# A banded attention block and its dense layer: no branch ahead of the work, other PSUM banks for the first chunk, other due times

## The chip, the cores and the metric

One core of a Trainium2 chip. The metric is device microseconds (us) of one execution of the program. Most executions agree within 0.3%.

## The reference: what is computed

```python
# attention: q, k, v are (4, 8, 768, 64) float32; n_sink = 4, window = 128 (int64 scalars)
scores = q @ k.T / sqrt(64)
keep = (key < n_sink) | ((query - key >= 0) & (query - key < window))
a = softmax(where(keep, scores, -1e9))        # divided by the row sum + 1e-9
x = (a @ v), laid out as (3072, 512)
# dense layer: w_in (512, 2048) and w_out (2048, 512), float64
h = x @ w_in
out = ((h * cos(h)) @ w_out).astype(float32)
```

`n_sink` and `window` are known only when the program runs. The kernel has a fast path for 0 <= n_sink <= 8 and 1 <= window <= 128, and a general path for everything else.

## The kernel before, in words

**Tiling.** The 3072 tokens are 12 chunks of 256 (`NT`), each of one batch. Per chunk there are 8 heads of attention and then 8 dense slots. A slot is 256 of the 2048 columns of `w_in`: 24 products for h (L393, half 0 needs head pairs 0 and 1 of x, half 1 the pairs 2 and 3), the cosine chain on ACT and DVE (L402 to L432), and 12 products into the two output accumulators (L441). Numbers are carried as a high and a low part (`xhi`, `xlo`, `whi`, `wlo`), so each product is three matmuls. The first three chunks (one of each of three batches, 24 heads, `o.early`) do their attention in plain float32 on TensorE: transposes of q and k (`qk`, L736), scores (`s`, L760), masked copy with row minimum (`p`, L829), exponential (L838), scaling (L858), transposes of p (`tp`, L918), values (`av`, L948). The other chunks use split operands (L816, L972).

**Weights.** They are float64 in memory. 32 pieces of 512 KB are loaded into one of two `raw` buffers; DVE makes a float32 of each in three instructions (L494, L500, L506), ACT rounds it to the high part (L527), DVE or POOL subtracts for the low part (L530). 32 more loads later feed a range check (`check_piece`), whose result `redo` says at the very end whether the general path must run.

**The order of the work** is written out ahead of time by a planner (`Plan`). Each step has engines with a cost each, its dependencies, and a due time (`prio`, smaller goes first); `order` walks through time, gives each free engine its ready step with the smallest due time, and the result is emitted engine by engine. On the chip each engine then goes through its own list in that order and waits by semaphores. The due times are built from the table `C`: `head_time(g)` and `slot_time(a, s)` are the base times, `DQ`, `DS`, `DX`, `DV`, `DA` shift the steps of a head, `WI`, `WO`, `WS`, `LEAD` those of the weights, `CK` those of the range check. With `FILL`, 160 matmuls into an unused bank (`idle`, L1208) stand in the plan with the last due time of all, so they take TensorE's planned gaps.

**PSUM** has eight banks: `s` (scores), `tp`, `av`, `b3` (`qk`), `b0` and `b1` (output accumulators), `b4` and `b2` (h of the slots in turn; `b3` too from the third chunk on).

**The opening.** `setup` loads `n_sink` and `window` on SP's queue, makes the identity, iotas and 22 warm-up matmuls (11 in the source, each runs as two), and has DVE compute whether the limits suit the fast path (`flag`). The planner's clock has a gate at 5.4: the loads on SP, and DVE and ACT steps marked `ahead`, may stand before it. All else comes behind a branch on `flag`: every engine loads the flag into a register (L1407) and branches (L1408). Behind the branch DVE makes the masks (L1258 to L1266) in among its first steps, and POOL clears three tiles.

**The end.** DVE reduces the range check to `redo` (L1278 to L1282, with one transpose on TensorE, L1280), every engine loads it (L1411) and branches past the general path (L1412).

Of the kernel before, what the change touches and what calls it, by code (L numbers as in the profile page):

```python
# [16 lines left out]
P = 128  # L17
NSINK = 8
# [28 lines left out]
class Plan:  # L47
# [5 lines left out]
    def __init__(self):  # L53
        self.steps, self.bufs, self.port, self.ahead = [], {}, set(), set()
# [6 lines left out]
    def add(self, engines, fn, deps, prio, lat=0.0, table=None, port=False, ahead=False):  # L61
        self.steps.append((engines, fn, deps, prio, lat, table))
        if ahead:
            self.ahead.add(len(self.steps) - 1)
        if port:
            self.port.add(len(self.steps) - 1)
        return len(self.steps) - 1

    def order(self, gate=0.0):
# [22 lines left out]
        free = dict.fromkeys(ready, gate)  # L92
        free["SP"] = min(gate, 0.9)
        free["DVE"] = free["ACT"] = min(gate, C["PRE"])
# [4 lines left out]
        table, done, starts = None, [False] * n, []  # L99
# [3 lines left out]
        while left:  # L103
# [4 lines left out]
            for e, rs in ready.items():  # L108
# [60 lines left out]
        early = gate - 1e-6  # L169
        return [s for s in starts if s[0] < early], [s for s in starts if s[0] >= early]  # L170
# [3 lines left out]
def attn_moe_kernel(ctx, tc, q, k, v, n_sink, window, w_in, w_out, out):  # L174
# [439 lines left out]
    def banded_path():  # L614
# [513 lines left out]
        def after_softmax(g, o):  # L1128
# [8 lines left out]
            if o.early:  # L1137
# [8 lines left out]
                if o.odd == 0:  # L1146
                    x.bav = buf("av", 1)
# [298 lines left out]
```

## Time and profile before

| | |
|---|---|
| three runs | 768.08, 768.29, 772.59 us; median 768.29 |
| the profiled execution | 770.14 us, span of its instructions 768.7 us |
| granted TensorE clock, mean | 0.989 |
| busy: TensorE matmul / DVE / ACT / POOL | 740.4 / 610.1 / 579.1 / 140.4 us |
| chain that ended last | PE 79%, DVE 7%, ACT 6%, DMA 5%, issue 2% |

Busy TensorE time includes the 160 `idle` matmuls and the warm-up, which compute nothing. Matmuls are pipelined, so a group's time from start to start is the better price of one. `PEclk` is the granted clock as a share of 2.4 GHz.

### The profile page before, as it was taken

The numbers are of one execution on the slowest core, as the hardware profiler recorded it, in microseconds if no ns is written. First come the engines' busy times: TensorE is split into PE (matmuls) and PEld (weight loads), VectorE is DVE, ScalarE is ACT, GpSimd is POOL, SyncE is SP. The second block draws the span as 40 slices with busy tenths as digits, with TensorE's granted clock in tenths as the row PEclk, the third lists the DMA queues.
The fourth block names the chain that finished last, engine by engine and source line by source line (L and its number), as shares of the span: only waits on it lengthen the run. The fifth ranks groups of instructions, "written<-read, shape, count | busy, mean of one in ns | idle before, by whom it ended". The sixth has DMA issues, their size and how long they took to land.

```text
span 768.7 us, 15296 instructions
## 1 busy us (share of the span) xinstructions
PE 740.4 (96%) x5027; PEld 669.1 (87%) x5027; DVE 610.1 (79%) x1606; ACT 579.1 (75%) x1350; POOL 140.4 (18%) x234
## 2 busy tenths in 40 slices
PE   7998979999999999999999999999999999999995
PEld 6787858899998999988989999999998999999994
DVE  5888889867898989989989987987878978954431
ACT  2798885868888778788787788798789888874331
POOL 2120220000122222222222312221022212210000
PEclk8999999999999999999999999999999999999998
DMA  5575465221374376375275342322323222110000
GB/s 154 163 199 155 155 159 176 58 43 36 77 185 101 62 181 159 66 196 129 51 191 153 60 111 50 52 66 51 57 58 63 53 62 52 35 40 1 28 1 32
DMA packets 215674, 71.51 MB, mean 93 GB/s; under 512 B 204320, under 2 KB 204320, under 8 KB 215584
## 3 DMA queue, kind: packets, MB, share of 16 engines
q1 hardware_dynamic: 215584, 70.43, 38.0%
q8 instruction: 42, 0.69, 0.4%
q14 instruction: 48, 0.39, 0.2%
HBM read 64.10 MB, written 6.29 MB: 92 GB/s over the span
## 4 chain that ended last, share of the span: by engine, by line
PE 79%; DVE 7%; ACT 6%; DMA 5%; issue 2%; SPq 1%; DVEq 0%
PE h L393 30%; PE acc L441 29%; PE av L972 5%; PE tp L918 4%; PE s L816 4%; DMA xk<-in_k_dram 2%; PE av L948 2%; PE idle L1208 1%; ACT p L838 1%; PE s L760 1%; DMA v<-in_v_dram 1%; DVE p L829 1%; DMA xq<-in_q_dram 1%; PE gp L900 1%; DVE glo L432 1%
## 5 line engine op out<-in xcount | busy, mean ns | idle before, releaser
L393 PE MATMUL h<-xhi,whi_in 128*128 128x256 f32 x768 | 224.4, 292 | 3.9 <-DVE glo L432 3.9
L393 PE MATMUL h<-xlo,whi_in 128*128 128x256 f32 x768 | 216.3, 282 | 0.0
L393 PE MATMUL h<-xhi,wlo_in 128*128 128x256 f32 x768 | 216.0, 281 | 0.0
L393 PEld LDWEIGHTS h<-xhi,whi_in 128*128 128x128 f32 x768 | 145.1, 189 | 15.2 <-DVE glo L432 5.9
L441 PE MATMUL acc<-whi_out,ghi 128*128 128x512 f32 x384 | 155.8, 406 | 0.2
L393 PEld LDWEIGHTS h<-xhi,wlo_in 128*128 128x128 f32 x768 | 145.4, 189 | 7.9 <-issue 0.5
L441 PE MATMUL acc<-wlo_out,ghi 128*128 128x512 f32 x384 | 151.7, 395 | 0.2 <-DVE wlo_out L530 0.2
L441 PE MATMUL acc<-whi_out,glo 128*128 128x512 f32 x384 | 150.7, 392 | 0.0
L393 PEld LDWEIGHTS h<-xlo,whi_in 128*128 128x128 f32 x768 | 145.1, 189 | 0.0
L829 DVE CUSTOM_DVE_ANT_0 p<-s,mk 128x264 f32<-128x264 f32 (+1 forms) x192 | 75.9, 399 | 28.1 <-PE s L816 22.3
L838 ACT ACTIVATE p<-p,st 128x264 f32<-128x264 f32 (+1 forms) x192 | 93.5, 490 | 0.7
L432 DVE TENSOR_TENSOR glo<-h,ghi 128x512 fp32r<-128x512 f32 x96 | 65.7, 684 | 30.3 <-ACT ghi L426 29.5
L441 PEld LDWEIGHTS acc<-whi_out,glo 128*128 128x128 f32 x384 | 72.3, 188 | 16.4
L415 ACT ACTIVATE r<-r,neg 128x512 f32<-128x512 f32 x96 | 69.0, 723 | 20.4 <-DVE r L408 20.0
L441 PEld LDWEIGHTS acc<-whi_out,ghi 128*128 128x128 f32 x384 | 72.7, 189 | 5.4 <-DVE raw L384 0.5
L441 PEld LDWEIGHTS acc<-wlo_out,ghi 128*128 128x128 f32 x384 | 73.0, 190 | 4.8 <-DVE wlo_out L530 0.7
L420 DVE TENSOR_TENSOR h<-h,r 128x512 f32<-128x512 f32 x96 | 66.1, 690 | 14.0 <-ACT r L415 13.8
L408 DVE SCALAR_TENSOR_TENSOR r<-h,yt 128x512 f32<-128x512 f32 x96 | 65.4, 682 | 14.4 <-ACT yt L402 13.8
L426 ACT CAST ghi<-h 128x512 fp32r<-128x512 f32 x96 | 55.8, 581 | 27.7 <-PE acc L441 26.7
L402 ACT ACTIVATE yt<-h 128x512 int32<-128x512 f32 x96 | 57.2, 596 | 19.6 <-PE h L393 18.1
L871 POOL TENSOR_TENSOR vr<-v,vr 128x192 fp32r<-128x192 f32 (+1 forms) x57 | 33.8, 592 | 159.6 <-ACT vr L866 145.1
L816 PE MATMUL s<-r,l 128*128 128x264 f32 (+2 forms) x288 | 61.0, 292 | 0.2
(128 smaller groups left out, 1381.5 us busy)
## 6 DMA issues: line engine op xcount, KB each, us to landing
raw<-in_moe_w_in_dram SPq DMA_DIRECT2D x32, 512.0 KB
raw<-in_moe_w_out_dram SPq DMA_DIRECT2D x32, 512.0 KB
xk<-in_k_dram SPq DMA_DIRECT2D x256, 48.0 KB
out_dram<-raw SPq DMA_DIRECT2D x24, 256.0 KB
v<-in_v_dram SPq DMA_DIRECT2D x64, 96.0 KB
xq<-in_q_dram SPq DMA_DIRECT2D x144, 32.0 KB
v<-in_v_dram SPq DMA_DIRECT2D x32, 64.0 KB
xq<-in_q_dram SPq DMA_DIRECT2D x24, 64.0 KB
```

Source lines behind the costliest of these rows:

```text
L393: nc.tensor.matmul(out=o.h[:, t, :], lhsT=w[:, c, fs], rhs=xx[:, c, :], start=(c == 0 and n == 0), stop=(c == NC - 1 and n == 2),)
L402: nc.scalar.activation(out=yt, in_=o.h, func=AF.Copy, scale=INV2PI, bias=0.25)
L408: nc.vector.scalar_tensor_tensor(out=o.r, in0=o.h, scalar=INV2PI, in1=yt, op0=ALU.mult, op1=ALU.subtract)
L415: nc.scalar.activation(out=o.r, in_=o.r, func=AF.Sin, scale=TWOPI_DOWN, bias=quarter)
L420: nc.vector.tensor_tensor(out=o.h, in0=o.h, in1=o.r, op=ALU.mult)
L426: nc.scalar.copy(out=o.ghi, in_=o.h)
L432: e.tensor_tensor(out=o.glo, in0=o.h, in1=f32(o.ghi), op=ALU.subtract)
L441: nc.tensor.matmul(out=x.acc[j], lhsT=gg[:, t, j * P : (j + 1) * P], rhs=w[:, f, :], start=(f == 0 and n == 0), stop=(f == NFT - 1 and n = ...
L816: nc.tensor.matmul(out=o.s_ps[j][:, :w], lhsT=o.l[:, j * P : (j + 1) * P], rhs=r.rearrange("p n s -> p (n s)")[:, c0 : c0 + w], start=(n = ...
L829: nc.vector.tensor_tensor_reduce(out=o.p[:, j, :w], in0=o.s_ps[j][:, :w], in1=masks[min(o.i0 + j, 2)][:, :w], op0=ALU.add, op1=ALU.min, sc ...
L838: nc.scalar.activation(out=o.p[:, j, :w], in_=o.p[:, j, :w], func=AF.Exp, bias=o.lead.st[:, 0, o.nth, j : j + 1], scale=-1.0, accum_out=o. ...
L972: nc.tensor.matmul(out=dst, lhsT=lhs, rhs=rhs, start=(n == 0), stop=(n == len(seq) - 1), skip_group_check=True)
```

## The change

The branch on `flag` goes. The fast path now always runs, and limits that do not suit it are joined to `redo`, so that the general path follows, as it does after a failed range check. The limits' loads go to ACT's queue; the conversion of the limits, the test on them and the masks become steps of the plan; the planner has one start time per engine (`BEGIN`) in place of the gate. The first q and k loads come before all weight loads. The clearing of tiles goes into `setup`, the 22 warm-up matmuls become 8. In the first chunk, the second score tile of a pair goes to `b1` and every second `tp` and `av` to `b4` and `b2`; `idle` moves from `b1` to `b0`. The reduction to `redo` becomes three steps of the plan behind the last range check. The float32 heads get due times of their own (`QE`, `SE`, `XE`, `VE`, `AE`, and `E`, `TE` for each chunk), and nearly all values of `C` change.

```diff
 C = {
-    "ALT": 2.669, "BLF": -0.052, "CK": 27.435, "DA": -3.097, "DH": -2.747, "DM": -0.791, "DQ": 10.525, "DS": -2.397,
-    "DV": 4.41, "DX": 7.018, "FILL": 160, "GHI": 2, "GLO": 2, "L": 1, "LAG": 4.21, "LEAD": 18.263, "NEH": 24,
-    "NM": 1.373, "NW": 2.093, "NWF": 0.026, "PB": 5, "PEN": 10.744, "PL": 3, "POOLF": 0.675, "POOLPEN": 2.303,
-    "PRE": 4.5, "R": 2, "RAW": 2, "SAME": 0.13, "SEM": 0.2, "SPE": 0.3, "STEP": 5.59, "T": 6.142, "TH": -1.227,
-    "WARM": 11, "WI": -18.566, "WO": 7.302, "WS": 1.56, "WS2": -0.177, "WT": 2, "XV": 2,
+    "AE": 0.079, "ALT": 2.961, "BLF": -0.149, "CK": 68.749, "DA": 0.079, "DH": -3.836, "DM": -1.983, "DQ": 5.572,
+    "DS": -1.813, "DV": 5.203, "DX": 4.169, "E": [0.0, -8.12, 37.201], "FILL": 160, "GHI": 2, "GLO": 2, "L": 1,
+    "LAG": 4.21, "LB": 49.088, "LEAD": 27.811, "NE": 0.98, "NEH": 24, "NM": 0.98, "NW": 3.409, "NWF": 0.067, "PB": 5,
+    "PEN": 8.817, "PL": 3, "POOLF": 1.838, "POOLPEN": 0.253, "QE": 5.572, "R": 2, "RAW": 2, "S0": -9.16, "S1": 47.611,
+    "SAME": -0.209, "SE": -1.813, "SEM": 0.31, "SPE": 0.11, "STEP": 6.272, "T": 6.142, "TE": [-1.145, 6.142, 6.142],
+    "TQ": 6.142, "VE": 5.203, "WARM": 4, "WI": -19.801, "WO": 7.156, "WS": 2.329, "WS2": 0.23, "WT": 2, "XE": 4.169,
+    "XV": 2,
 }
-GATE = 5.4
+BEGIN = {"PE": 3.4, "ACT": 0.7, "POOL": 2.6, "DVE": 2.3, "SP": 0.8}
...
     def setup():
-        nc.sync.dma_start(out=nw_i[:, 0, :], in_=n_sink.unsqueeze(0).broadcast_to([P, 2]))
-        nc.sync.dma_start(out=nw_i[:, 1, :], in_=window.unsqueeze(0).broadcast_to([P, 2]))
...
-        nc.gpsimd.memset(redo, 1)
+        nc.gpsimd.memset(env.kz, 0.0)
         nc.gpsimd.memset(xb, 0.0)
+        nc.gpsimd.memset(env.gc, 0.0)
+        nc.gpsimd.memset(f32(env.vs), 0.0)
+        for _ in range(C["WARM"]):
+            nc.tensor.matmul(out=env.warm, lhsT=ident, rhs=ident, start=True, stop=True)
...
+    def load_limits(e):
+        nc.scalar.dma_start(out=nw_i[:, 0, :], in_=n_sink.unsqueeze(0).broadcast_to([P, 2]))
+        nc.scalar.dma_start(out=nw_i[:, 1, :], in_=window.unsqueeze(0).broadcast_to([P, 2]))
+        nc.scalar.activation(out=flag[:, 2:3], in_=quarter[0:1], func=AF.Exp)
+    def limits(e):
         nc.vector.tensor_copy(out=nw4, in_=nw_i)
-        nc.vector.tensor_tensor(out=lims[:, 0], in0=nw4[0:1], in1=lims[:, 0], op=ALU.is_ge)
-        nc.vector.tensor_tensor(out=lims[:, 1], in0=nw4[0:1], in1=lims[:, 1], op=ALU.is_le)
         nc.vector.tensor_single_scalar(out=neg, in_=nw4[:, :, 0], scalar=0.0, op=ALU.is_lt)
-        nc.vector.tensor_tensor(out=lims[:, 0], in0=lims[:, 0], in1=lims[:, 1], op=ALU.mult)
-        nw_hi = nw4[:, :, 1]
-        nc.vector.tensor_tensor(out=nw_hi, in0=nw_hi, in1=neg, op=ALU.add)
+        nc.vector.tensor_tensor(out=neg, in0=nw4[:, :, 1], in1=neg, op=ALU.add)
+        nc.vector.scalar_tensor_tensor(
+            out=neg, in0=neg, scalar=4294967296.0, in1=nw4[:, :, 0], op0=ALU.mult, op1=ALU.add
+        )
+    def beyond(e):
+        nc.vector.tensor_tensor(out=lims[:, 0], in0=nw4[0:1], in1=lims[:, 0], op=ALU.is_lt)
+        nc.vector.tensor_tensor(out=lims[:, 1], in0=nw4[0:1], in1=lims[:, 1], op=ALU.is_gt)
...
+        def masked(m):
+            nc.vector.tensor_scalar(out=m, in0=m, scalar1=-1.0, scalar2=MASKED, op0=ALU.add, op1=ALU.mult)
+        def mask_0(e):
+            nc.vector.tensor_scalar(out=diag, in0=rel, scalar1=wd_f, scalar2=None, op0=ALU.is_lt)
+            nc.vector.scalar_tensor_tensor(out=diag, in0=rel, scalar=0.0, in1=diag, op0=ALU.is_ge, op1=ALU.mult)
+            nc.vector.tensor_scalar(out=cols, in0=col, scalar1=ns_f, scalar2=None, op0=ALU.is_lt)
+            nc.vector.tensor_tensor(out=m0, in0=cols, in1=diag, op=ALU.max)
+            masked(m0)
+        def mask_1(e):
+            nc.vector.tensor_copy(out=mb[:, P:SW], in_=cols[:, :NSINK])
+            nc.vector.tensor_scalar(out=prev, in0=rel, scalar1=float(P), scalar2=wd_f, op0=ALU.add, op1=ALU.is_lt)
+            nc.vector.tensor_tensor(out=cols, in0=cols, in1=prev, op=ALU.max)
+            nc.vector.tensor_copy(out=ma[:, P:], in_=diag)
+            masked(ma)
+        def mask_2(e):
+            masked(mb)
...
+        i = add([("ACT", 1.9)], load_limits, [], -3000.0, lat=2.8)
+        i = add([("DVE", 0.6)], limits, [i], -3000.0, lat=0.1)
+        add([("DVE", 0.4)], beyond, [i], C["LB"])
+        mks = [add([("DVE", 1.2)], mask_0, [i], -3000.0, port=True)]
+        mks.append(add([("DVE", 1.4)], mask_1, mks[:], -2999.0, port=True))
+        mks.append(add([("DVE", 0.3)], mask_2, mks[1:], C["LB"], port=True))
...
-        start = H * C["TH"]
-        start2 = start + NSLOT * C["STEP"]
         def head_time(g):
-            return g * C["TH"] if g < H else start2 + (g - 2 * H) * T
+            a, h = divmod(g, H)
+            return C["E"][a] + h * C["TE"][a] if a < NE else C["S1"] + (g - (NE - 1) * H) * T
         def slot_time(a, s):
-            return start2 + ((a - 1) * NSLOT + s) * T if a else start + s * C["STEP"]
+            return C["S1"] + ((a - 1) * NSLOT + s) * T if a else C["S0"] + s * C["STEP"]
...
+            o.s_banks, o.tp_bank, o.av_bank = ("s", "s"), "tp", "av"
+            if o.a == 0:
+                o.s_banks, o.tp_bank, o.av_bank = ("s", "b1"), ("tp", "b4")[o.odd], ("av", "b2")[o.pair % 2]
...
-                    i = add(dma(2), load_natural(xq_t, src, CB), [bx], t - 8 * T + C["DQ"] + 0.4, lat=2.3)
+                    i = add(dma(2), load_natural(xq_t, src, CB), [bx], t - 8 * T + DQ + 0.4 if g else -2000.0, lat=2.3)
-                    i = add(dma(2), load_natural(xk_t, src, o.nkb), [bx], t - 7 * T + C["DQ"] + 1.2, lat=2.4)
+                        dma(2), load_natural(xk_t, src, o.nkb), [bx], t - 7 * T + DQ + 1.2 if g else -1999.0, lat=2.4
...
-                    bs = buf("s", 1)
+                    bs = buf(o.s_banks[j], 1)
...
-                p0 = add([("PE", 0.107 * o.n)], turn(o), o.nm + [pt], t + C["DA"] + 1.3)
+                pt, bpt = buf(o.tp_bank, 1), buf("phi", 1)
...
-                    x.bav = buf("av", 1)
+                    x.bav = buf(o.av_bank, 1)
...
+        def least_all(e):
+            e.tensor_reduce(out=tmin[:, 0:1], in_=tiny, axis=mybir.AxisListType.X, op=ALU.max)
+        def least_turn(e):
+            env.tm = ps.tile([1, P], F32, name="tm", tag="tp")
+            e.transpose(out=env.tm, in_=tmin[:, 0:1], identity=ident)
+        def least_flag(e):
+            e.tensor_reduce(out=tmin[0:1, 1:2], in_=env.tm, axis=mybir.AxisListType.X, op=ALU.max)
+            e.scalar_tensor_tensor(
+                out=redo, in0=tmin[0:1, 1:2], scalar=-MIN_TOP * MIN_TOP, in1=flag[:, 0:1], op0=ALU.is_gt, op1=ALU.max
+            )
-        idle = buf("b1", 1)
+        idle = buf("b0", 1)
...
-        first_loads, steps = plan.order(GATE)
-        emit(first_loads, setup)
-        yield
...
-        emit(steps)
...
+            t = slots[8 + 2 * NSLOT + len(checks)][0]
+            btp = buf("tp", 1)
+            i = add([("DVE", 0.16)], least_all, checked, t)
+            i = add([("PE", 0.13)], least_turn, [i, btp], t + 1.0)
+            btp.users.append(add([("DVE", 0.4)], least_flag, [i], t + 2.0))
+        emit(plan.order(BEGIN), setup)
...
-    fast = banded_path()
-    next(fast)
-    banded = nc.values_load(flag.bitcast(I32)[:, 1:2], min_val=0, max_val=1)
-    with tc.If(banded > 0):
-        with ExitStack() as ctx2:
-            next(fast)
...
+    with ExitStack() as ctx2:
+        banded_path()
```

## Rows read from the trace of the kernel before

**Rows 1.** By stretch: from:to, length, busy us and count, PEclk, DMA share, GB/s.

```profile
0.00:7.48 7.48, 4.05 (x22) 3.86 (x22) 1.74 (x16) 0.07 (x1) 1.40 (x10) 1.00 0.43 133
7.48:14.88 7.40, 5.31 (x25) 5.26 (x26) 6.04 (x16) 3.56 (x6) 2.43 (x4) 0.54 0.58 128
14.88:60.00 45.12, 43.22 (x290) 36.94 (x289) 38.31 (x122) 34.23 (x107) 6.64 (x8) 1.00 0.62 177
60.00:160.00 100.00, 90.34 (x551) 77.11 (x550) 86.61 (x200) 79.30 (x178) 11.68 (x14) 0.98 0.49 137
160.00:300.00 140.00, 138.29 (x966) 126.40 (x965) 115.14 (x314) 112.12 (x257) 28.10 (x45) 1.00 0.46 105
300.00:740.00 440.00, 439.34 (x3074) 402.65 (x3074) 355.78 (x931) 343.65 (x794) 90.17 (x154) 1.00 0.33 74
```

**Rows 2.** The same stretches, `idle` matmuls (L1208) alone.

```profile
7.48:14.88 7.40, 4.71 (x19) 4.26 (x20) 0.54 0.58 128
14.88:60.00 45.12, 23.24 (x142) 18.54 (x140) 1.00 0.62 177
60.00:160.00 100.00, 0.37 (x1) 0.19 (x1) 0.98 0.49 137
```

**Rows 3.** Timeline of the opening, DVE and ACT: start, length, instruction, idle time before.

```profile
5.82 0.17 DVE L256 CAST nw<-nw_i 128x4 f32<-128x4 int32 x1 [3.66 <-DMA nw_i<-in_window_dram]
...
7.41 1.28 ACT L382 ACT_TABLE_LOAD   x1 [7.41 <-DVE flag L269]
...
7.48 0.46 DVE L494 TENSOR_SCALAR wt<-raw 128x512 int32<-128x512 int32 x1 [0.70 <-DMA raw<-in_moe_w_in_dram]
...
8.90 0.68 DVE L494 TENSOR_SCALAR wt<-raw 128x512 int32<-128x512 int32 x1 [0.95 <-DMA raw<-in_moe_w_in_dram]
...
9.63 0.29 DVE L1258 TENSOR_SCALAR mk<-yt,neg 128x128 f32<-128x128 f32 x1
...
14.88 0.29 DVE L829 CUSTOM_DVE_ANT_0 p<-s,mk 128x128 f32<-128x128 f32 x1 [0.35 <-PE s L760]
```

**Rows 4.** Timeline of TensorE in the same time.

```profile
9.57 0.66 PE L736 MATMUL qk<-ident,xq 128*128 128x128 f32 x2 [4.16 <-DMA xq<-in_q_dram]
...
11.38 2.91 PE L1208 MATMUL idle<-gt 128*128 128x256 f32 x12
14.08 0.76 PE L760 MATMUL s<-kz,tq 128*128 128x256 f32 x2
```

**Rows 5.** Chain of waits, first long step: start, length, what.

```profile
3.07 6.36 DMA xq<-in_q_dram
```

**Rows 6.** Timeline of SP's issues.

```profile
1.18 0.42 SPq L234 DMA_DIRECT2D nw_i<-in_window_dram  x1
1.65 0.90 SPq L486 DMA_DIRECT2D raw<-in_moe_w_in_dram  x2
2.59 0.95 SPq L728 DMA_DIRECT2D xq<-in_q_dram  x2
```

**Rows 7.** Waits of DVE up to 60 us: engine, line, releaser, sum, times, longest.

```profile
DVE p L829 <- PE s L760: 2.9, 5, 1.2
DVE wt L494 <- DMA raw<-in_moe_w_in_dram: 2.4, 3, 1.0
```

**Rows 8.** Chain of waits at the first dense slot.

```profile
58.08 1.43 PE h L393 x12
```

**Rows 9.** L1411, L1412: count, duration min/median/max ns, first, last start.

```profile
L1411 SPq TENSOR_LOAD <-redo x1: 731/731/731, 761.0 to 761.0; - x1
...
L1412 PEldq COMPARE_BRANCH  x1: 3655/3655/3655, 760.9 to 760.9; - x1
...
L1412 SPq COMPARE_BRANCH  x1: 45/45/45, 761.8 to 761.8; - x1
```

**Rows 10.** Waits of SP after 755 us.

```profile
SPq L1412 <- SPq L1412: 3.6, 1, 3.6
```

**Rows 11.** Timeline of SP after 756 us.

```profile
759.05 1.69 SPq L457 DMA_DIRECT2D out_dram<-raw  x2
```

More of the change, by code (lines that the diff above doesn't have):

```diff
@@ L53, in __init__ @@
     def __init__(self):
-        self.steps, self.bufs, self.port, self.ahead = [], {}, set(), set()
+        self.steps, self.bufs, self.port = [], {}, set()
     def buf(self, tag, n):
@@ L59, in buf, with add @@
         return row[-1]
-    def add(self, engines, fn, deps, prio, lat=0.0, table=None, port=False, ahead=False):
+    def add(self, engines, fn, deps, prio, lat=0.0, table=None, port=False):
         self.steps.append((engines, fn, deps, prio, lat, table))
-        if ahead:
-            self.ahead.add(len(self.steps) - 1)
         if port:
@@ L91, in order @@
         ready = {e: set() for e in ("PE", "ACT", "POOL", "DVE", "SP")}
-        free = dict.fromkeys(ready, gate)
-        free["SP"] = min(gate, 0.9)
-        free["DVE"] = free["ACT"] = min(gate, C["PRE"])
+        free = dict(begin or dict.fromkeys(ready, 0.0))
         events = [(0.0, i) for i in range(n) if not wait[i]]
@@ L98, in order @@
         heapq.heapify(wake)
-        table, done, starts = None, [False] * n, []
+        table, done, starts = "exp" if begin else None, [False] * n, []
         now = 0.0
@@ L168, in order @@
                 now = wake[0]
-        early = gate - 1e-6
-        return [s for s in starts if s[0] < early], [s for s in starts if s[0] >= early]
+        return starts
 @with_exitstack
@@ L514, in flush @@
                 )
-            s1 = add((("DVE", dve(WP, True)),), shift, [last, bt], prio, port=True, ahead=True)
-            s2 = add((("DVE", dve(WP)),), top, [s1], prio, port=True, ahead=True)
-            s3 = add((("DVE", dve(WP)),), low, [s2], prio, port=True, ahead=True)
+            s1 = add((("DVE", dve(WP, True)),), shift, [last, bt], prio, port=True)
+            s2 = add((("DVE", dve(WP)),), top, [s1], prio, port=True)
+            s3 = add((("DVE", dve(WP)),), low, [s2], prio, port=True)
             r.users += [s1, s2, s3]
@@ L530, in rest_lo @@
             e.tensor_tensor(out=lo, in0=t32, in1=f32(hi), op=ALU.subtract)
-        s4 = add((("ACT", act(WP)),), round_hi, [last], prio, ahead=True)
+        s4 = add((("ACT", act(WP)),), round_hi, [last], prio)
         s5 = add(sub(WP), rest_lo, [s4], prio, port=True)
@@ L617, in banded_path @@
         T = C["T"]
+        ap = env.ap = ctx2.enter_context(tc.tile_pool(name="ap", bufs=1))
+        ps = env.ps = ctx2.enter_context(tc.tile_pool(name="ps", bufs=1, space=PSUM))
+        mk = ap.tile([P, 3 * P + BW], F32, name="mk")
+        masks = m0, ma, mb = mk[:, :P], mk[:, P : 3 * P], mk[:, 3 * P :]
+        diag, prev, cols = mb[:, SW:], mb[:, :P], ma[:, :P]
+        gc = env.gc = ap.tile([P, CB, GR], F32, name="gc")
+        vs = env.vs = ap.tile([P, NP, 2, 2, D], F32R, name="vs")
+        env.kz = ap.tile([P, 2, NT], F32, name="kz", tag="plo")
+        env.warm = ps.tile([P, P], F32, name="warm", tag="b0")
+        def masked(m):
[14 more added lines that the diff above has]
+            masked(mb)
         heads = []
@@ L912, in fn @@
             def fn(e):
[L913 removed]
+                o.tp = ps.tile([P, 4 * P], F32, name=f"tp_{o.tag}", tag=o.tp_bank)
                 n = 0
@@ L940, in fn @@
                 if o.odd == 0:
-                    x.f[o.pair] = ps.tile([P, 2, NT], F32, name=f"av_{o.tag}", tag="av")
+                    x.f[o.pair] = ps.tile([P, 2, NT], F32, name=f"av_{o.tag}", tag=o.av_bank)
                 mms = []
@@ L1045, in before_softmax @@
                             [("ACT", act(o.nkb * P, False)), ("DVE", dve(o.nkb * P))], k_out(o, half),
-                            [i] + (kk or ([o.bkz] if g else [o.bkz, bkz])), t - 6 * T + C["DQ"] + 1.6 + 0.01 * half,
+                            [i] + (kk or ([o.bkz] if g else [o.bkz, bkz])), t - 6 * T + DQ + 1.6 + 0.01 * half,
                         ))
@@ L1155, in after_softmax @@
                 x.sums[o.pair] = [y0]
-                x.bav.users += split_x(plan, x, o.a, o.pair, t + C["DA"] + 5.0, o.odd)
+                x.bav.users += split_x(plan, x, o.a, o.pair, t + DA + 5.0, o.odd)
                 return
             bvr = buf("vr", 1)
-            v0 = add([("ACT", act(o.nkb * D))], v_hi(o), [i, bvr], t - T + C["DV"] + 3.0)
-            v1 = add(sub(o.nkb * D), v_lo(o), [v0], t - T + C["DV"] + 3.2, port=True)
+            v0 = add([("ACT", act(o.nkb * D))], v_hi(o), [i, bvr], t - T + DV + 3.0)
+            v1 = add(sub(o.nkb * D), v_lo(o), [v0], t - T + DV + 3.2, port=True)
             bx.users += [v0, v1]
@@ L1190, in after_softmax @@
             bxb = buf("xb", 1)
-            y1 = add([("ACT", act(NT, False))], x_low(o), [y0, bxb], t + C["DA"] + 4.8)
+            y1 = add([("ACT", act(NT, False))], x_low(o), [y0, bxb], t + DA + 4.8)
             if o.odd == 0:
                 x.bf = buf("x", 1)
-            y2 = add([("DVE", dve(NT))], x_sum(o, x), [y0, y1] + (x.sums[o.pair] or [x.bf]), t + C["DA"] + 5.1)
+            y2 = add([("DVE", dve(NT))], x_sum(o, x), [y0, y1] + (x.sums[o.pair] or [x.bf]), t + DA + 5.1)
             bav.users += [y1, y2]
@@ L1206, in fn @@
                 if n == 0:
-                    env.idle = ps.tile([P, 2, P], F32, name="idle", tag="b1")
+                    env.idle = ps.tile([P, 2, P], F32, name="idle", tag="b0")
                 nc.tensor.matmul(
@@ L1287, in banded_path @@
-        yield
+        if w64:
+            t = slots[8 + 2 * NSLOT + len(checks)][0]
[4 more added lines that the diff above has]
+        emit(plan.order(BEGIN), setup)
+        if not w64:
+            nc.vector.tensor_copy(out=redo, in_=flag[:, 0:1])
     def general_path():
```

122 lines of the change are left out of this document (43 added, 79 removed).

## The prediction, made before the changed kernel was built or run

> **What bounds the kernel now.** I read the busy time by stretch first, then the same stretches for the `idle` matmuls alone. From 160 us to 740 us TensorE is busy without a break: 138.29 of 140 us and 439.34 of 440 us [rows 1]. There the end is set by TensorE's work, which the change leaves as it is. Before that TensorE waits. Up to 60 us its real work is busy time less `idle` and warm-up: 0.60 us between 7.48 and 14.88 (5.31 - 4.71) and 19.98 us between 14.88 and 60 (43.22 - 23.24), so 20.6 of 60 us [rows 1, 2]. From 60 to 160 us it does 89.97 us, a gap of 10.03 [rows 1, 2]. In the same stretches DVE is busy 82%, 85% and 87% (6.04 of 7.40, 38.31 of 45.12, 86.61 of 100) and ACT 48%, 76% and 79% [rows 1]. So the first 160 us belong to DVE more than to any other engine, with a part left to latency, and a microsecond won there moves the start of the full stretch by as much. The timeline shows how the opening is spent. DVE gets the limits at 5.82 us, its first weight instruction starts at 7.48, the next one waits 0.95 us for a load, and the first masked scores start at 14.88 [rows 3]. TensorE's first transpose waits until 9.57 us for q [rows 4], whose load took 6.36 us behind two weight loads [rows 5].
>
> **The change part by part.** The working is against the profiled execution (770.14 us, 768.7 of it span) and is carried to the median of 768.29 as a difference; the 1.85 us between the two are taken to be in both kernels.
>
> *The opening on DVE.* Today the limits land 5.82 us into the span, 4.2 us after the end of their second issue at 1.60 [rows 3, 6]. On ACT's queue, which is empty then, the two issues end at about 0.7 + 2 x 0.42 = 1.5, so I take the same landing. Four of the nine instructions on the limits stay ahead of the masks, about 0.5 us, so mask work starts at 6.3 where ordinary work started at 7.48: 1.1 us. The waits of 0.95 us (second weight piece) and 0.35 us (first scores) [rows 3] are filled by masks, which by then have their inputs: 1.3 us. Against that stand two more mask instructions of about 0.29 us [rows 3], 0.5 us less what one wide one gave back. Sum for DVE: 1.9 us earlier. The price hangs on the landing, because conversion and masks go first in DVE's list: all else on DVE (weight pieces, masked scores, copies out of `qk`) is queued behind them, and ACT's rounding behind that.
>
> *The opening as latency.* SP issues the two q loads first, 0.95 us for the pair [rows 6], from 0.8 us, then k, then the first weight pieces from about 2.7 where they went at 1.65; these land some 1.1 us later than today (8.5 and 10 us), the first behind the masks, the second with up to 0.8 us left to wait unless masked scores fill it. With the 4.2 us of the limits' loads as landing time, q is there by 6 us and k by 7; with the 6.36 us of today's q load 2 us later. From the first transpose to the scores took 4.5 us (9.57 to 14.08), of it 2.9 us twelve `idle` matmuls [rows 4], at a granted clock of 0.54 over the stretch, close to the lower level of 1.2 GHz [rows 1]: the engine had stood still for 4.16 us before its first transpose [rows 4]. The masks are ready at about 6.3 + 5 x 0.29 = 7.7 and, for the wider tile, 9.2. So masked scores start between 7.7 and 9.3, at least 5.6 us before 14.88. How much of this reaches the end lies between 1.9 us (DVE is the limit) and 5.6 us (the chain of the heads is). DVE is busy 85% of the stretch that follows, which speaks for the lower end, and the gaps in it for more than that; I take the middle, **3.8 us**.
>
> *Banks.* DVE waits for `s` 2.9 us in all up to 60 us, of which 0.35 is counted above [rows 7, 3]. One of the two score tiles of a pair gets its own bank, so TensorE can write it while the other is still read. Half of 2.55 us: **1.3 us**, between 0 and 2.55. The bill comes with the first dense slot: its h stands in `b4`, which odd heads now use to the last. Today half of that h is done in a gap before x is complete; in `b4` it follows the last `tp`, twelve matmuls or 1.43 us [rows 8] more at that point. DVE has weight pieces to do in that time, so it costs nothing; without that cover 1.4 us.
>
> *Weight loads.* `LEAD` grows from 18.3 to 27.8, so loads are issued sooner; DVE waited 2.4 us for them, 0.95 of it counted above [rows 7, 3]. Half of the 1.45 left: **0.7 us**, between 0 and 1.45. A load waits for its buffer as before, and that is late next.
>
> *POOL's clearings* move ahead of the branch point; POOL is busy 1.40 of the first 7.48 us [rows 1], which covers them. ACT's two issues (0.8 us) and its table load (1.28 us) move to a time when ACT does nothing until 7.41 [rows 3]. The three steps for `redo` and the test on the limits cost TensorE and DVE under 1 us in a full stretch: **-0.1 us**.
>
> *The end.* Today TensorE's sequencer spends 3.66 us in the branch past the general path, after `redo` [rows 9]. With `redo` known long before, it can take that branch while its last matmuls run. By that row alone the end would come up to 2.7 us sooner (SP's branch is at 761.8, TensorE's is over at 764.6), and the forecast would be 759.9. But SP waits 3.6 us behind its own branch [rows 9, 10], to 765.5, and its load of `redo` at 761.0 follows its last store issue, which ends at 760.74 [rows 11]. So I take 0, and 0.3 us as the other bound. The Trainium skill (Runtime: NRT & Kernel Launch, Instruction fetch mechanics) says that a taken branch to a far target makes the engine fetch before it goes on. By that rule every engine pays and the gain is 0; SP's 3.6 us agree.
>
> *Due times.* Chunk 1's slots start 56.8 behind chunk 0's in place of 44.7; chunk 2's heads come 10.4 ahead of chunk 1's slots in place of level with them; the range check moves back by 41 into a stretch where DVE has 84 us free (440 - 355.78) [rows 1]. Such a re-ordering can fill the gap of 10.03 us or widen it. I count 0 and make the two ends rivals.
>
> Sum: 3.8 + 1.3 + 0.7 - 0.1 = 5.7 us, so 768.3 - 5.7 = **762.6 us**. Its own range is 758.8 to 766.5, with all terms at their upper and at their lower bounds.
>
> **The rivals.** *The gap closes too.* Chunk 2's heads bring float32 work to TensorE before chunk 1's slots are due, and weights come sooner. If 8 of the 10.03 us go, 754.6. For it: 13.4 us of idle DVE in that stretch [rows 1]. Against: DVE at 87% and ACT at 79% leave little.
>
> *The opening is swallowed.* The limits land as late as q does today: 1.5 + 6.4 = 7.9, and ordinary DVE work starts at 8.4, 0.9 us later than 7.48; that and the 0.5 us for masks eat the 1.3 us of waits filled, and half of the bank and load terms, 1.0 us, is left. That gives 767.3. For it: q, k and limits now come to the same transfer engines within two microseconds. Against: today two weight loads stood ahead of q, and now none does. The Trainium skill (Trainium Kernel Development and Optimization, Key Constraints) says that the queues of SP and ACT run on the same DMA engines and interleave, and that a second issuer saves only issue time; that rule points to this case, and no row of this trace shows two queues at once.
>
> *Slower: the slots of chunk 1 come too late.* Between chunk 0's last slot and chunk 1's first the due times leave a hole. If heads do not fill it, TensorE stands still for the 12.1 by which chunk 1's slots are put back: 762.6 + 12.1 = 774.7. It decides where the gap from 60 to 160 us grows from 10.03 to over 16 us. Against it: a ready step is taken whatever its due time, so a hole opens only where DVE does head work in place of slot work.
>
> **How the numbers follow.** Chances: forecast 0.50, gap closes 0.27, swallowed 0.15, slower 0.08. Over 1% faster, about the least that a measurement of this kernel can tell from no change, is under 760.6: 0.15 of the forecast's 0.50, and all of the second case: 0.42. Slower than 776.0 is a little over half of the last case: 0.05. Within 1%: 0.53. The range runs from 752 (the second case with all of the gap gone gives 752.6) to 769.5; under it lie some 0.06, above it 0.08.
>
> **What would show it.** Right: the first masked scores before 9.5 us, the first transpose before 6.5, `s` no longer leading DVE's waits up to 60 us, the full stretch of TensorE beginning 5 to 6 us earlier, an end that is as long as today. Wrong: the limits landing after 7 us, the gap of TensorE from 60 to 160 us far from 10 us on either side, or an end shorter by 2 us or more.

## The result and the profile after

The changed kernel took 761.4 us (median; 760.48 to 762.47) where the kernel before took 768.25 beside it: a ratio of 0.9886 [0.986, 0.9913]; the two medians alone give 0.991. The forecast was 762.6, in a range of 752 to 769.5. The total came out near; several terms of the sum did not, and that is what the rest is about.

The profiled run of the changed kernel took 762.47 us, 760.5 of it span (768.7 before). First its busy time by stretch, with the columns of [rows 1]:

```profile
0.00:7.48 7.48, 5.98 (x27) 5.42 (x28) 3.15 (x18) 1.86 (x3) 2.99 (x12) 1.00 0.53 134
7.48:14.88 7.40, 7.31 (x54) 6.49 (x54) 5.42 (x18) 2.23 (x6) 0.18 (x1) 1.00 0.45 120
14.88:60.00 45.12, 38.88 (x240) 32.40 (x239) 39.22 (x118) 36.99 (x115) 5.53 (x5) 0.96 0.66 190
60.00:160.00 100.00, 93.47 (x580) 80.35 (x579) 90.06 (x197) 80.66 (x189) 10.38 (x11) 1.00 0.46 132
160.00:300.00 140.00, 138.97 (x977) 127.79 (x976) 121.54 (x333) 115.12 (x268) 22.32 (x39) 1.00 0.45 103
300.00:740.00 440.00, 438.92 (x3077) 403.24 (x3076) 359.95 (x959) 332.92 (x778) 63.01 (x107) 1.00 0.33 74
```

The `idle` matmuls of the same stretches (they are L1262 now):

```profile
0.00:7.48 7.48, 3.59 (x15) 3.21 (x16) 1.00 0.53 134
7.48:14.88 7.40, 6.32 (x45) 5.54 (x46) 1.00 0.45 120
14.88:60.00 45.12, 16.04 (x103) 13.35 (x101) 0.96 0.66 190
```

Less these and 2.08 us of warm-up, TensorE is busy for 24.1 us by 60 us, against 20.6 before [rows 1, 2]: 3.5 more. That is not yet 3.5 us more of work. `idle` and real matmuls overlap in time, so taking off all the time of `idle` takes off time of real ones too. Counted from 0 to 60 us, 154 real matmuls stand there before (335 less 159 `idle` and 22 of warm-up) and 149 after (317 less 160 and 8). An estimate without the subtraction prices every real matmul by the median time from its start to the next start, for its kind, at the full clock, over all the traces of this case. By it the work begun is as follows, with a second profile from the repeat of the changed kernel below:

| begun by | 60 us | 160 us | 740 us |
|---|---|---|---|
| kernel before | 25.6 | 111.2 | 683.4 |
| changed kernel | 25.1 | 115.2 | 689.5 |
| its second profile | 27.7 | 117.2 | 691.5 |

So by 60 us the gain is nothing in one profile, whose clock falls there (last section), and 2.1 us in the other. From 60 to 160 us it is 4.5 and 3.9 us. TensorE's busy time there is 93.47 us against 89.97, and the gap has gone from 10.03 to 6.53 us. From 160 to 740 us the busy time hardly changes (+0.7, then -0.4), and the estimate finds 2.1 us more. What is left after 740 us shows the rest, first for the kernel before, then for the changed one:

```profile
740.00:768.70 28.70, 19.87 (x108) 16.91 (x106) 6.47 (x11) 6.16 (x10) 0.00 (x0) 0.88 0.07 22
```

```profile
740.00:760.50 20.50, 13.76 (x70) 11.41 (x68) 3.37 (x5) 4.15 (x7) 0.00 (x0) 0.94 0.09 31
```

TensorE has 6.1 us less to do after 740 (19.87 - 13.76), and the time there in which it does nothing is 2.1 us shorter (8.83 to 6.74). 6.1 + 2.1 is the 8.2 us by which the span fell. The measured time of the two executions fell by 7.7 (770.14 to 762.47): 1.4 us of it lay outside the span before, 2.0 after.

The opening, from the timeline of the changed kernel on ACT, SP and DVE (columns of [rows 3]):

```profile
0.74 0.43 ACTq L249 DMA_DIRECT2D nw_i<-in_n_sink_dram  x1
1.19 0.45 ACTq L250 DMA_DIRECT2D nw_i<-in_window_dram  x1
...
0.74 0.96 SPq L755 DMA_DIRECT2D xq<-in_q_dram  x2
...
2.77 0.94 SPq L483 DMA_DIRECT2D raw<-in_moe_w_in_dram  x2
...
5.06 0.17 DVE L254 CAST nw<-nw_i 128x4 f32<-128x4 int32 x1 [2.73 <-DMA nw_i<-in_window_dram]
5.86 0.28 DVE L630 TENSOR_SCALAR mk<-yt,neg 128x128 f32<-128x128 f32 x1
...
9.59 0.29 DVE L856 CUSTOM_DVE_ANT_0 p<-s,mk 128x128 f32<-128x128 f32 x1 [1.27 <-PE s L787]
```

And on TensorE, without the `idle` matmuls:

```profile
5.44 0.66 PE L763 MATMUL qk<-ident,xq 128*128 128x128 f32 x2
7.19 0.38 PE L763 MATMUL qk<-ident,xk 128*128 128x128 f32 x2
8.96 1.45 PE L787 MATMUL s<-kz,tq 128*128 128x256 f32 x4
```

The limits land 3.4 us after their second issue ends (5.06 - 1.64), not 4.2; the first transpose is at 5.44 in place of 9.57 [rows 4], and the first masked scores at 9.59 in place of 14.88 [rows 3]. DVE's waits up to 60 us (columns of [rows 7]) are now led by `s`; before, the wait for the limits, 3.66 us [rows 3], stood ahead of the 2.9 for `s`:

```profile
DVE p L856 <- PE s L787: 3.4, 3, 1.4
DVE nw L254 <- DMA nw_i<-in_window_dram: 2.7, 1, 2.7
DVE wt L491 <- DMA raw<-in_moe_w_in_dram: 2.1, 4, 0.7
```

The end, from the lines of the branch and of the load of `redo` (columns of [rows 9]):

```profile
L1432 SPq EVENT_SEMAPHORE  x8: 17/17/17, 758.6 to 759.1; - x8
...
L1461 DVEq EVENT_SEMAPHORE  x2: 21/21/21, 759.9 to 760.5; - x2
...
L1432 PEldq COMPARE_BRANCH  x1: 3562/3562/3562, 750.2 to 750.2; - x1
...
L1432 SPq COMPARE_BRANCH  x1: 45/45/45, 755.1 to 755.1; - x1
...
L1431 SPq TENSOR_LOAD <-redo x1: 464/464/464, 695.0 to 695.0; - x1
```

The last store issues, from the timeline of SP (columns of [rows 11]):

```profile
753.06 1.69 SPq L454 DMA_DIRECT2D out_dram<-raw  x2
```

And three more lines of the kernel before:

```profile
L1412 SPq EVENT_SEMAPHORE  x8: 17/17/17, 765.5 to 766.0; - x8
...
L1411 SPq FUSED_REGOPS  x1: 169/169/169, 766.1 to 766.1; - x1
...
L1441 DVEq EVENT_SEMAPHORE  x2: 21/21/21, 767.1 to 768.6; - x2
```

TensorE's branch, 3.56 us long, now lies under its last matmuls, and SP loads `redo` 60 us ahead of its branch. SP still waits 3.5 us behind its own branch (755.1 to 758.6). But that branch follows the end of the last store issue (754.75) by 0.35 us, where 1.06 us with a load of `redo` of 0.73 us stood between (760.74 to 761.8) [rows 9, 11]: 0.7 us. From the last of SP's eight semaphores to the end it is 1.4 us (759.1 to 760.5) where it was 2.7 (766.0 to 768.7). Before, SP had a check of the loaded register to do there (766.1), and the last semaphore of DVE came at 768.6, for which the trace gives no reason.

### The profile page after: what moved, and what is told of

Its sections match the earlier page's. It is cut to its first block, busy times and chain, and to the rows that moved or that the text cites. A ratio compares the mean times of both kernels' runs of the same rounds, so it can differ in the third digit from the quotient of the medians.

```text
span 760.5 us, 15290 instructions
## 1 busy us (share of the span) xinstructions
PE 737.3 (97%) x5013; PEld 667.1 (88%) x5013; DVE 622.7 (82%) x1645; ACT 573.9 (75%) x1361; POOL 104.4 (14%) x174
## 4 chain that ended last, share of the span: by engine, by line
PE 78%; DVE 10%; ACT 5%; DMA 3%; issue 2%; SPq 0%; POOL 0%; DVEq 0%; POOLq 0%; ACTq 0%
PE h L390 30%; PE acc L438 29%; PE av L999 5%; PE s L843 4%; PE tp L945 4%; DVE wt L503 2%; ACT p L865 2%; DVE wt L497 2%; PE idle L1262 1%; DVE p L856 1%; PE gp L927 1%; PE s L787 1%; DMA raw<-in_moe_w_out_dram 1%; DMA raw<-in_moe_w_in_dram 1%; PE av L975 1%
## 5 line engine op out<-in xcount | busy, mean ns | idle before, releaser
L438 PE MATMUL acc<-whi_out,ghi 128*128 128x512 f32 x384 | 159.0, 414 | 0.0
L865 ACT ACTIVATE p<-p,st 128x264 f32<-128x264 f32 (+1 forms) x192 | 93.5, 488 | 0.5
L898 POOL TENSOR_TENSOR vr<-v,vr 128x192 fp32r<-128x192 f32 (+1 forms) x47 | 29.0, 617 | 215.3 <-ACT vr L893 175.1
```

Source lines behind the costliest of these rows:

```text
L438: nc.tensor.matmul(out=x.acc[j], lhsT=gg[:, t, j * P : (j + 1) * P], rhs=w[:, f, :], start=(f == 0 and n == 0), stop=(f == NFT - 1 and n = ...
L865: nc.scalar.activation(out=o.p[:, j, :w], in_=o.p[:, j, :w], func=AF.Exp, bias=o.lead.st[:, 0, o.nth, j : j + 1], scale=-1.0, accum_out=o. ...
```

## The experiments

All ratios are to the kernel before, timed beside each kernel. 0.001 is 0.77 us. The intervals are 0.002 to 0.003 to either side, so a difference of less than some 2.5 us between two experiments is not shown by the times alone.

**The changed kernel again.**

> The changed kernel again, beside the others on the same chip: 760.5 to 762.5 us, 6 to 8 us under the kernel before. It is the zero for the differences below.

It took 760.56 us, 0.9881 [0.9859, 0.9904]. In its profile TensorE is busy with real work for 25.4 us by 60 us (by the subtraction) and for 92.96 from 60 to 160. The two sets of the changed kernel, 0.9886 and 0.9881, are 8.8 to 9.1 us under the kernel before.

**Structure without due times.** The changed kernel, with the due times and planner costs of before in its table.

```diff
-"E": [0.0, -8.12, 37.201], "S0": -9.16, "S1": 47.611, "LEAD": 27.811, ...
+"E": [0.0, -14.232, 34.904], "S0": -9.816, "S1": 34.904, "LEAD": 18.263, ...
```

> The changed structure (no first branch, limits and masks as plan steps, first q and k loads ahead, other banks, redo in the plan) with the due times and planner costs of the kernel before. Theory 'opening': the structure carries the gain. Then 762 to 764.5 us: the opening's 2 to 4 us and the shorter end (from the last store issue to the end of the span 5.75 us in place of 7.96, so 2.2 us). Rival 'due times': the new order carries it. Then only the end's 2.2 us show and it is 765.5 to 767.5 us.

It took 766.47 us, 0.9941 [0.9917, 0.9964]: 4.5 us of the 9, inside the band of the rival "due times". Its windows:

```profile
14.88:60.00 45.12, 40.90 (x269) 34.48 (x268) 37.71 (x121) 36.39 (x112) 7.87 (x7) 1.00 0.64 183
60.00:160.00 100.00, 89.24 (x545) 75.82 (x544) 88.39 (x201) 79.89 (x176) 16.91 (x22) 1.00 0.49 137
160.00:300.00 140.00, 137.58 (x969) 126.56 (x968) 110.88 (x302) 115.11 (x259) 34.56 (x54) 1.00 0.47 109
300.00:740.00 440.00, 435.86 (x3052) 399.64 (x3051) 350.06 (x925) 347.25 (x797) 89.51 (x149) 1.00 0.33 72
```

By 60 us TensorE has been busy with real work for 25.0 us, 4.4 more than before (3.3 more by the estimate, 28.9 against 25.6). Then it loses 0.7, 0.7 and, in the stretch that had been full, 3.5 us (439.34 to 435.86): what the opening won is given back late. By 740 us the estimate stands at 683.4 us, the same as before.

**Due times without structure.** The kernel before, with the changed kernel's due times and costs.

```diff
-return g * C["TH"] if g < H else start2 + (g - 2 * H) * T
+return C["E"][a] + h * C["TE"][a] if a < NE else C["S1"] + (g - (NE - 1) * H) * T
```

> The kernel before with the due times and planner costs of the changed one; branch, gate, banks, warm-up and end as before. Theory 'opening': 766.5 to 770 us, no gain beyond 2 us. Rival 'due times': 762 to 765 us. If each theory has half, both this kernel and the structure alone lie near 765 us, and their gains add up to the whole; if the two need one another, both lie above 766.

It took 766.47 us, 0.9958 [0.994, 0.9975]: 3.2 us. Its opening is the old one (first masked scores at 14.24), and the work from 60 to 300 us is denser:

```profile
60.00:160.00 100.00, 95.38 (x583) 81.27 (x584) 90.47 (x209) 80.86 (x184) 12.73 (x15) 0.98 0.47 132
160.00:300.00 140.00, 139.58 (x971) 127.56 (x970) 121.79 (x334) 114.67 (x267) 21.16 (x36) 1.00 0.45 102
300.00:740.00 440.00, 438.61 (x3081) 403.48 (x3080) 360.19 (x961) 334.13 (x781) 64.81 (x111) 1.00 0.33 75
```

The gap from 60 to 160 us is 4.6 in place of 10.03. Both kernels lie above 766 us, the sign that was named for two parts that need one another; but 4.5 and 3.2 make 7.7 us of the 8.8 to 9.1, which the intervals do not tell from a plain sum.

**The reduction to `redo` back at the end.**

```diff
-i = add([("DVE", 0.16)], least_all, checked, t)
-i = add([("PE", 0.13)], least_turn, [i, btp], t + 1.0)
-btp.users.append(add([("DVE", 0.4)], least_flag, [i], t + 2.0))
 ...
+least_all(nc.vector); least_turn(nc.tensor); least_flag(nc.vector)   # after the plan
```

> The changed kernel with the reduction to redo moved back to the very end, as it stood before. Theory: SP's load of redo, which now runs 59 us before the end, moves back behind the last store, and the span from the last store issue to the end grows from 5.75 to about 8 us: 763 to 764 us, 2.0 us (1.5 to 2.5) over the changed kernel. Rival: the shorter end is chance or belongs to the missing first branch; then within 0.5 us of the changed kernel.

It took 763.25 us, 0.9901 [0.988, 0.9922]: 2.7 us over the changed kernel's median beside it, 1.5 by the ratios. The lines of its end:

```profile
L1433 SPq EVENT_SEMAPHORE  x8: 17/17/17, 763.7 to 764.2; - x8
...
L1433 PEldq COMPARE_BRANCH  x1: 3522/3522/3522, 758.4 to 758.4; - x1
...
L1433 SPq COMPARE_BRANCH  x1: 45/45/45, 759.4 to 759.4; - x1
...
L1432 SPq TENSOR_LOAD <-redo x1: 498/498/498, 758.2 to 758.2; - x1
```

And of its timeline of SP:

```profile
756.48 1.69 SPq L454 DMA_DIRECT2D out_dram<-raw  x2
```

The last store issue ends at 758.17 and the span at 765.6: 7.4 us, against 5.7 in the changed kernel (754.75 to 760.5) and 8.0 before (760.74 to 768.7). By the times an early `redo` is worth 1.5 to 2.7 us, which lies within their noise. The traces settle it: from the last store issue to the end of the span it takes 4.9 to 5.9 us in all nine profiled runs with an early `redo`, and 6.8 to 8.0 us in all five with a late one.

**The bank alternation taken out.**

```diff
-o.s_banks, o.tp_bank, o.av_bank = ("s", "b1"), ("tp", "b4")[o.odd], ("av", "b2")[o.pair % 2]
+o.s_banks, o.tp_bank, o.av_bank = ("s", "s"), "tp", "av"
```

> The changed kernel, with one score bank (s), one tp and one av bank for the first chunk's heads as before; all else is the changed kernel. Theory (the bank term of the forecast): DVE's waits for s up to 60 us grow again, by 0 to 2.55 us, and the end comes 1.3 us later: 762.3 where the unedited one measured 761.0 over its two sets of runs. Rival (banks bought nothing, since s still leads DVE's waits at 3.4 us with the second bank): within 0.7 us of 761.0, with DVE's waits for s unchanged. A second rival (the planner fills the wait with other work, and the bank moves real TensorE work from one stretch to another): TensorE's real work up to 60 us falls by 1 us or more, but the end stays within 0.7 us.

It took 767.18 us, 0.9942 [0.9918, 0.9965]: 4.3 to 4.7 us worse than the changed kernel by the ratios, above the forecast's 0 to 2.55, though the intervals reach down to some 2.2. DVE's waits for `s` rise only from 3.4 (2.8 in the second profile of the changed kernel) to 4.4 us; the work from 60 to 160 us falls from 93.0 or 93.5 to 91.16:

```profile
60.00:160.00 100.00, 91.16 (x566) 78.29 (x566) 90.10 (x198) 79.83 (x180) 11.51 (x16) 1.00 0.46 133
```

The granted clock differs too: its mean over these ten runs is 0.992, over the nine of the changed kernel 0.996. The one run here with 0.996 took 763.75 us, where the changed kernel's three runs with 0.996 took 760.62 to 762.82. How much of the loss is waits and how much the clock is not separated.

**Only one part of the alternation.** `s` in one bank, `tp` and `av` alternating; then the other way round.

```diff
+o.s_banks, o.tp_bank, o.av_bank = ("s", "s"), ("tp", "b4")[o.odd], ("av", "b2")[o.pair % 2]
```

> The changed kernel with one score bank for the first chunk's heads (both tiles of a pair in s); tp and av still alternate. Theory (the forecast's place: the score bank is the one that pays): as with all banks undone, ratio 0.993 to 0.996, DVE's waits for s up to 60 us 4 us or more. Rival (tp and av banks pay): within 0.0015 of 0.9884.

```diff
+o.s_banks, o.tp_bank, o.av_bank = ("s", "b1"), "tp", "av"
```

> The changed kernel with two score banks for the first chunk's heads, but one tp and one av bank, as before. Theory (the score bank pays): within 0.0015 of 0.9884. Rival (tp and av banks pay): 0.993 to 0.996, with TensorE's waits for tp or av between 14.88 and 160 us longer by 2 us or more.

They took 761.06 us, 0.9878 [0.9848, 0.9907], and 761.0 us, 0.9869 [0.9841, 0.9897]. Neither theory holds for both: either half alone is as good as the whole. A second bank for `s`, or second ones for `tp` and `av` together, is enough, and the score bank, on which the forecast put the term, is not needed for it. With one score bank DVE's waits for `s` up to 60 us were 2.5 us, not 4 or more. Why either half serves, the runs do not show.

**The alternation alone,** in the kernel before (the same lines, and the `idle` matmuls moved to `b0`).

> The kernel before, with the change's alternation of banks for the first chunk's heads (and the idle matmuls moved to b0, since b1 is now a score bank); opening, due times and end are those of before. Taking the banks out of the changed kernel cost 0.0056 of its time (0.9942 where the two sets of the changed kernel gave 0.9881 and 0.9886). Theory (banks are a term of their own, about three times the forecast's 1.3 us): ratio to the kernel before 0.9925 to 0.996, 3 to 6 us. Rival (the forecast's size): 0.997 to 1.000, at most 2.5 us. Second rival (banks are worth something only with the new due times): 0.999 to 1.001.

It took 768.14 us, 0.9975 [0.9957, 0.9993]: 1.9 us, inside the band of the rival, the forecast's size. By 160 us it is well ahead, then it gives back 2.0 us of a stretch that had been full (439.34 to 437.34), as the structure without due times does:

```profile
60.00:160.00 100.00, 94.23 (x590) 81.77 (x590) 91.22 (x213) 81.45 (x179) 10.17 (x12) 1.00 0.48 138
...
300.00:740.00 440.00, 437.34 (x3063) 401.18 (x3062) 349.45 (x920) 346.89 (x796) 89.10 (x149) 1.00 0.33 72
```

**Due times and alternation, old opening and old end.**

> The kernel before with the new due times and planner costs and with the alternation of banks; the old opening (limits first on SP's queue, nine instructions and a branch ahead of the heads) and the old end stay. What is missing against the changed kernel is the opening and the end alone. Theory (the opening earns nothing, as 2.4 us of later first scores cost nothing): due times 0.0042 and banks 0.0056 add up, ratio 0.989 to 0.9915, the rest to 0.9884 being the end. Rival (the forecast's opening of 3.8 us, between 1.9 and 5.6): 0.993 to 0.998.

It took 766.9 us, 0.9943 [0.9922, 0.9963], inside the band of the rival: due times and banks did not add up to the theory's 0.989 to 0.9915. What is missing against the changed kernel is 4.4 to 4.8 us; less 1.5 to 2.7 for the end, the opening is worth 1.7 to 3.3 us. These are differences of middle values; their intervals allow anything from nearly nothing to more than the forecast's 3.8.

**The first weight loads back in front of q and k.** The two fixed due times of the first loads are taken away.

```diff
-t - 8 * T + DQ + 0.4 if g else -2000.0
+t - 8 * T + DQ + 0.4
```

> The changed kernel, with the first two weight loads in front of the first q and k on SP's queue again (the fixed head-of-list due times of that one load pair are taken away); limits, masks and banks stay as changed. Theory (the opening is a chain of latencies): first transpose back near 9 us (5.44 with q first), first masked scores near 13 us in place of 9.6, TensorE's real work up to 60 us down by 2 us or more, the end 1.5 to 4 us later: 762.5 to 765. Rival (DVE sets the opening; it has masks and, sooner, weight pieces to do): first masked scores late all the same, but the end at most 1.0 us later, 761 to 762, and real work up to 60 us down by less than 1.5 us.

It took 761.26 us, 0.9875 [0.9845, 0.9905]. It ends no later, though its opening is later, as its timeline shows:

```profile
6.27 0.43 DVE L491 TENSOR_SCALAR wt<-raw 128x512 int32<-128x512 int32 x1 [3.94 <-DMA raw<-in_moe_w_in_dram]
...
8.07 0.17 DVE L254 CAST nw<-nw_i 128x4 f32<-128x4 int32 x1 [0.64 <-DMA nw_i<-in_window_dram]
...
11.96 0.29 DVE L856 CUSTOM_DVE_ANT_0 p<-s,mk 128x128 f32<-128x128 f32 x1 [0.63 <-PE s L787]
...
8.60 0.41 PE L763 MATMUL qk<-ident,xq 128*128 128x128 f32 x2 [1.56 <-DMA xq<-in_q_dram]
```

The first transpose comes 3.2 us later and the first masked scores 2.4 us later, and yet TensorE has been busy with real work for 25.4 us by 60 us, as long as in the second profile of the changed kernel (28.0 and 27.7 by the estimate). DVE begins a weight piece before the limits land, and is less late than the scores are:

```profile
0.00:7.48 7.48, 5.62 (x23) 5.06 (x23) 2.10 (x9) 1.49 (x2) 2.99 (x12) 1.00 0.59 168
7.48:14.88 7.40, 6.28 (x47) 5.78 (x48) 5.81 (x26) 2.19 (x6) 0.00 (x0) 1.00 0.30 66
```

By 14.88 us DVE has done 7.91 us of work (2.10 + 5.81) against 8.57 in the changed kernel (3.15 + 5.42), 0.66 less. The theory that the opening is a chain of latencies falls, with room for some 2 us in the intervals. That DVE's work sets it fits, but it is not shown by itself: the plan was worked out anew, so the order behind the opening differs too.

**The limits on SP's queue,** in front of q and k; ACT keeps its table load.

```diff
-nc.scalar.dma_start(out=nw_i[:, 0, :], ...)
+nc.sync.dma_start(out=nw_i[:, 0, :], ...)
```

> The changed kernel, with the two limits loads issued by SP in front of q and k in place of ACT; ACT keeps its table load only. Theory (a queue of its own saves issue time alone, 0.9 us for q): limits land within 0.5 us of the 5.06 us at which DVE took them, the first transpose comes 0.9 us later (6.3), first masked scores 0.5 to 1.0 later, the end 0 to 1 us later: 761 to 762. Rival (the two queues hold each other up today, so that loads on one queue land sooner): limits taken before 4.6 us, and the end no later than 761.

It took 763.68 us, 0.9898 [0.9869, 0.9928]. DVE takes the limits at 4.62 us, the first transpose is at 6.61, the first masked scores at 10.06. That lies between theory and rival, and the ratio is 1 us worse, which the intervals do not separate from nothing.

**220 `idle` matmuls in place of 160.**

```diff
-"FILL": 160
+"FILL": 220
```

> The changed kernel, with 220 idle matmuls at hand in place of 160; the plan is worked out anew with them, so the order of real work after about 47 us differs too. Theory (the granted clock of 0.50 at 56 to 58 us in one of the two profiles comes from TensorE standing still once the idle matmuls have run out): clock 0.95 or more in every 2 us from 46 to 60, slot 0's 12 h matmuls in 1.3 to 1.5 us in place of 2.56, the end 0 to 1.2 us earlier: 759.8 to 761. Rival (idle matmuls hold their bank and stand in front of real ones, so slot 0 starts later): real work up to 60 us down by 0.5 us or more, and the end 0 to 1.5 us later: 761 to 762.5.

It took 762.77 us, 0.9889 [0.9859, 0.9919]. The clock is 1.00 up to 160 us, as the theory had it. The subtraction gives 22.8 us of real work by 60 us, 1.3 to 2.6 less, the rival's sign; but here 30.56 us of `idle` are taken off, with what they overlap, in place of 25.95 and 26.20. By count 165 real matmuls stand there (367 less 194 and 8), between the 149 and 171 of the changed kernel's two profiles, and the estimate gives 27.0 us: the loss is not shown. The end is not shown to differ. No kernel of these is shown to be faster than the changed one.

## Why the prediction was right, and where its steps were not

The forecast case was right in its total (762.6 for 761.4), and its sum was right in part by luck: 5.7 us forecast, 6.9 measured between the medians (8.8 to 9.1 by the ratios), with two terms put at nothing that were not, and others off. Two of the signs named for a wrong forecast came: an end 2.2 us shorter, and a gap of 6.5 us from 60 to 160 us. Two numbers of its working are off as well. Its 20.6 us of real work by 60 us come from the subtraction and are too few (25.6 by the estimate), and the 758.8 of its own range leaves out the 0.3 us that it gave the end as a bound.

*The opening, 3.8 us.* The events came as forecast: limits at 5.06 (5.7 expected), first transpose before 6.5, first masked scores 0.09 us past the 9.5 named as the sign. By the middle values the term was too high: 1.7 to 3.3 us with banks and due times beside it, and next to nothing without banks (0.9942 with opening, due times and end, where due times alone gave 0.9958 and the end accounts for the difference) or under the old due times (4.5 us for the structure, less 1.9 for banks and 1.5 to 2.7 for the end). The intervals do not exclude 3.8. The weak step is the middle between 1.9 us (DVE) and 5.6 us (latency): in the weights-first kernel 2.4 us of latency cost nothing that the times show. By these values the lower bound was the one to take, and the row that said so was DVE's 85%.

*Banks, 1.3 us.* In size it held alone (1.9 us). Its reason did not: `s` still led DVE's waits, and a second bank for `tp` and `av` serves as well as one for `s`. Under the new due times it is worth 1.2 us with the old opening (0.9958 to 0.9943) and 4.3 to 4.7 us with the new one, part of that perhaps by the clock; the difference of the two is at the edge of the intervals. The slot 0 bill was called covered; no run shows it uncovered.

*Weight loads, 0.7 us.* Not tried alone. DVE's wait for them fell from 2.4 [rows 7] to 2.1 us, and to 1.5 in the second profile.

*The end, 0.* Wrong: 1.5 to 2.7 us by the times, 1.9 by the means of the nine and five traces. The row that was read, SP's 3.6 us behind its branch [rows 10], stands after the change too (3.5). What went stands around it: SP's load of `redo`, which had to come after the last store issue and ahead of the branch (0.7 us by the rows), and 1.3 us behind the wait, of which 1.0 (the late semaphore of DVE) is not explained. With the late `redo`, the load is back ahead of SP's branch and the wait behind it is 4.3 us. The forecast's "by TensorE's row alone", 2.7 us, was nearer, though not for its reason: TensorE's branch is hidden now, and SP's sets the end.

The Trainium skill (Runtime: NRT & Kernel Launch, Instruction fetch mechanics) says that a taken branch out of the fetched pages makes the engine wait for a fetch. TensorE's 3.56 us and SP's 3.5 us agree. That every engine pays it at the end did not follow: TensorE, which knew its condition early, paid it beside its matmuls (750.2 to 753.8 us).

*Due times, 0, with two rivals.* About 3.2 us. "The gap closes" was half true: 3.0 to 3.5 of its 8 us from 60 to 160. With the end, that is the missing term that stood in for the opening's overestimate. And the due times do more than fill that gap: under the old ones the opening's and the banks' gains were given back from 300 to 740 us (435.86 and 437.34 of 440), under the new ones that stretch stays at 438.6 to 439.8. So the parts need not add up as the forecast added them.

*"The opening is swallowed"* failed on its condition: the limits landed at 5.06, not 7.9. In the weights-first kernel they did land at 8.07, and even there the end was no later. *"Chunk 1's slots too late"* failed: the gap fell instead of growing past 16 us.

## What to carry to other kernels

Where one engine is 85% busy, as DVE is here, expect from a shorter chain of latencies in front of it only the work that it lets that engine do sooner; cost such an edit by the busy engine's instructions, not by the time at which something first appears. Look for where a gain would be given back: a stretch that is full today is full for today's arrivals. And when a wait at the end looks fixed, ask which work stands ahead of it and behind it, and whether that work's inputs exist earlier. Do not take the time of filler instructions off an engine's busy time where they overlap with real ones: count the real ones.

## What the runs showed of the hardware

**A stall of TensorE can be followed by a fall of its clock.** Windows of 4 us of the kernel before, where `tp` waits 3.2 us for ACT's `p`:

```profile
108.00:112.00 4.00, 1.67 (x5) 1.33 (x6) 3.27 (x9) 3.42 (x7) 3.81 (x5) 0.75 0.90 239
112.00:116.00 4.00, 4.00 (x14) 2.69 (x13) 3.38 (x9) 3.55 (x10) 0.23 (x1) 0.82 0.45 111
```

Then the changed kernel, once its `idle` matmuls have run out:

```profile
48.00:52.00 4.00, 2.33 (x16) 2.15 (x16) 3.74 (x12) 3.59 (x15) 0.00 (x0) 1.00 0.75 225
52.00:56.00 4.00, 2.13 (x10) 1.48 (x9) 3.85 (x12) 3.93 (x13) 0.58 (x1) 0.84 0.68 183
56.00:60.00 4.00, 4.00 (x20) 3.49 (x20) 2.90 (x9) 2.22 (x7) 0.00 (x0) 0.74 0.53 168
```

In both the engine does little, and then the granted clock falls toward the lower level of 1.2 GHz and is still low when the engine is fully busy again: in each case 1.7 us of the clock are lost (4 x 0.25 + 4 x 0.18; 4 x 0.16 + 4 x 0.26). Slot 0's twelve h matmuls took 2.56 us at that place, 1.43 before [rows 8]. In the second profile of the same kernel, with the same instructions, the clock stayed at 1.00 there; TensorE was busy 3.01 of the 4 us from 52 to 56 in it, 2.13 here. Whether it falls differs from run to run, and the times go with it: of the twelve runs with old opening, new due times and banks, the shortest (762.31 us) has a mean clock of 0.996 and the longest (770.41) 0.990. How much of that is the clock and how much the stall that lowers it is open; 220 `idle` matmuls kept the clock at 1.00 up to 160 us, and no gain from it is shown.

**Loads on one queue hold up those on another.** With two weight loads of 128x1024 first on SP's queue, the limits on ACT's own queue were taken at 8.07 us in place of 5.06, though they were issued from 0.74 to 1.64 us in both. The Trainium skill (Trainium Kernel Development and Optimization, Key Constraints) says that these queues run on the same engines and that a second issuer saves issue time alone; the 3 us agree.
